# Float64 weights by bit masks and ScalarE, key moments from 512 keys, and a new table of places

## The chip, the cores and the metric

The kernel runs on one core of a Trainium2 chip (trn2) as one program. The metric is the device time of an execution in microseconds (us). Engines are PE (matmul, transposes; writes PSUM), DVE (VectorE), ACT (ScalarE), POOL (GpSimd) and SP, which here only issues DMAs. Each engine works through its own queue in order and waits on semaphores for the others.

## The reference

Attention over 8 batches x 8 heads of 576 tokens with 64 dimensions, which keeps the 32 largest scores of each row, and behind it a layer with SoLU activation. `q`, `k`, `v` and `g_ln` are float32; `w_in` (512 x 1024) and `w_out` (1024 x 512) come as float64.

```python
scores = np.matmul(q, k.transpose(0, 1, 3, 2)) / np.sqrt(64)
kth = np.partition(scores, -32, axis=-1)[..., -32:-31]
scores = np.where(scores >= kth, scores, -1e9)
attn = np.exp(scores - scores.max(-1, keepdims=True))
attn = attn / (attn.sum(-1, keepdims=True) + 1e-9)
x = np.matmul(attn, v)            # (B, H, S, D) -> (B*S, H*D) = 4608 x 512
h = x @ w_in
solu = h * softmax(h)             # over 1024
ln = (solu - solu.mean(-1)) / np.sqrt(solu.var(-1) + 1e-6) * g_ln
out = ln @ w_out
```

## The kernel before

The work is cut into 32 **pairs** (a batch and two of its heads). A pair has nine score tiles of 128 queries x 576 keys: four row blocks for each of two heads (`j` = 0 to 7), and a ninth that holds the last 64 queries of both. Behind each batch come four **token tiles** of 128 tokens, and behind every second batch a **tails tile** with the last 64 tokens of two batches: 36 tiles through both weight matrices.

For a pair, in the order of the data (engine in brackets):

- `load_qk`, `load_v` [SP] bring q, k and v; `prep_t`, `prep_m` [PE] transpose q and k, and `prep_tc`, `prep_mc` [ACT] copy them to SBUF.
- `moments` [PE] multiplies the keys by themselves in bf16: per head a 64 x 64 matrix, over four blocks of main keys and a fifth with the last 64 (`kt`). `moments_c` [ACT], `spread` [PE], `spread_v` and `spread_r` [DVE] and `first_p` [POOL, with a power of 2.2 us] make of it the spread of each query's scores, and `first` [DVE] the first guess of the threshold.
- `scores` [PE] and `evac` [ACT] put the scores into SBUF. `count0` [DVE] counts those above the guess, `second` [DVE] improves it; `count1` [ACT, a sign with an accumulator], `third` [DVE]; `count2` [ACT].
- `side`, `nearest` (a product and MAX8) and `kth` [DVE] find the 32nd largest score among the eight nearest to the last guess.
- `exps` [ACT], `keep` [DVE] and `inverse` [DVE], `norm` [POOL] make the probabilities; `transpose_p`, `transpose_last` [PE] with `copy_p`, `copy_pt`, `copy_last` [ACT], and `attn_v` [PE] with `copy_v` [ACT] the result.

A token tile goes through `mm1` [PE, two halves], `hexp` [ACT], `solu` [DVE], `square` [ACT], `ln` [POOL], `transpose_ln` [PE] and `copy_ln` [ACT], `mm2` [PE, two halves] and `store` [ACT, then SP].

The **weights** are 16 chunks of 128 x 512, eight of `w_in` and eight of `w_out`. `load_w` brings 512 KB of float64; `finish_w` is a generator whose three steps are taken one at a time (`weights_step`). In `float64_stages` DVE masks exponent (L31) and mantissa (L34), POOL scales both (L37, L40, L43); DVE adds the low word (L47), POOL multiplies (L50); DVE sets the sign (L52). A chunk of `w_out` is then multiplied by `g_ln` on POOL (L563).

The **order** is written out by hand: tables give each function a place (`pair_times` and so on), a pair's places are moved by 39 per pair, and all calls are sorted by place. That order is the program order of PE, ACT, DVE and POOL; a place is no time.

```python
    with tc.manual_schedule(engines={E.PE, E.Activation, E.DVE, E.Pool}):
        for _, _, f, args in sorted(todo, key=lambda x: x[:2]):
            f(*args)
```

Buffers that matter below: the pool `p1` holds one tile of tag `e` (`hexp`'s result, or a chunk's helper), `p2` two of `solu` (also a chunk's `w_tmp`) and two of `lnT` (also `w_raw`); `ps_big` two PSUM tiles for scores, `spread` and `mm1`.

This is the fast path. At its end sums over range tests of the intermediate values decide (`bad`) whether a **general path** computes everything again.

Of the kernel before, what the change touches and what calls it, by code (L numbers as in the profile page):

```python
# [8 lines left out]
F32 = mybir.dt.float32  # L9
I32 = mybir.dt.int32  # L10
U32 = mybir.dt.uint32
AF = mybir.ActivationFunctionType
ALU = mybir.AluOpType
AX = mybir.AxisListType

P = 128
# [427 lines left out]
def fast_path(  # L444
# [22 lines left out]
    nc = tc.nc  # L467
    B, H, S, D = q.shape
    NTOK, DM = out.shape
    DFF = moe_w_in.shape[1]  # L470
    NM = 4
    SM = NM * P
# [4 lines left out]
    NT = 2 * NM + 1  # L477
    NG = NT // 3
    SP = S // 2
    scale = 1.0 / float(D) ** 0.5  # L480
    Z0 = 1.593
# [4 lines left out]
    const = ctx.enter_context(tc.tile_pool(name="const", bufs=1))  # L486
    p1 = ctx.enter_context(tc.tile_pool(name="p1", bufs=1))
    p2 = ctx.enter_context(tc.tile_pool(name="p2", bufs=2))
# [3 lines left out]
    small = ctx.enter_context(tc.tile_pool(name="small", bufs=3))  # L492
# [21 lines left out]
    den_all = const.tile([P, NPAIR, NT], F32, tag="den", name="den_all")  # L514
    NTT = NTOK // P
    sum_all = const.tile([P, NTT], F32, tag="sum", name="sum_all")
    w_in = const.tile([P, NP, DFF], F32, tag="w_in", name="w_in")
    w_out = const.tile([P, NF, DM], F32, tag="w_out", name="w_out")
    g_rows = const.tile([NF, P], F32, tag="g_rows", name="g_rows")
# [2 lines left out]
    def trunc(ap):  # L522

        return ap.bitcast(BF16)[:, 1::2]

# [6 lines left out]
    for c in range(NF):  # L534
        w_chunks.append((w_out[:, c, :], moe_w_out[c * P : (c + 1) * P, :], c))
    w_raw = {}

    def load_g():
        nc.sync.dma_start(out=g_rows, in_=moe_g_ln.rearrange("(c p) -> c p", p=P))
# [8 lines left out]
            dst = w_raw[n]  # L548
        nc.sync.dma_start(out=dst, in_=src)

    def finish_w(n):

        dst, _, c = w_chunks[n]
        if w_wide:
            tmp = p2.tile([P, 2, 512], F32, tag="solu", name="w_tmp")
            mi = p1.tile([P, DFF], F32, tag="e", name="w_mi")
            yield from float64_stages(
                nc, dst, w_raw.pop(n), tmp[:, 0, :].bitcast(I32),
                mi[:, 0:512].bitcast(U32), tmp[:, 1, :],
            )  # L560
        if c is not None:

            nc.gpsimd.tensor_scalar(  # L563
                out=dst, in0=dst, scalar1=g_col[:, c : c + 1], scalar2=1.0,
                op0=ALU.mult, op1=ALU.mult,
            )

    w_gen = [finish_w(n) for n in range(len(w_chunks))]

    def weights_step(n):  # L570

        next(w_gen[n], None)

    st = [dict() for _ in pairs]
    xs = {}

    def once(d, key, make):

        if key not in d:
            d[key] = make()
        return d[key]

    def columns(i, tag, n=NT):

# [80 lines left out]
    def moments(i):  # L667
        d = st[i]
        tm = d["tm"] = pre_of(i)[:, 2 * ST : 2 * ST + D]
        for c in range(NM + 1):  # L670
            for h in range(2):
                kc = trunc(d["k"][:, 2 * c + h, :] if c < NM else d["kt"][:, h, :])
                nc.tensor.matmul(
                    out=tm[h * D : (h + 1) * D, :], lhsT=kc, rhs=kc,
                    start=(c == 0), stop=(c == NM),
                )

    def moments_c(i):
# [44 lines left out]
    def first_p(i):  # L723
        d = st[i]
        zs = d["zs"] = small.tile([P, NT], F32, tag="zs", name="zs")
        nc.gpsimd.tensor_scalar(
            out=zs, in0=d["ss"], scalar1=(Z0 * scale) ** 2 / S, scalar2=0.0,
            op0=ALU.mult, op1=ALU.add,
        )
        nc.gpsimd.tensor_tensor(out=zs, in0=zs, in1=phalf.broadcast_to([P, NT]), op=ALU.pow)  # L730
        d["tb"] = small.tile([P, NT], F32, tag="tb", name="tb")
        nc.gpsimd.tensor_scalar(
            out=d["tb"], in0=zs, scalar1=GAIN, scalar2=1.0, op0=ALU.mult, op1=ALU.mult
        )
# [339 lines left out]
    def at(time, f, *args):  # L1074
        todo.append((time, len(todo), f, args))


    pair_times = [
        (load_qk, [()], [-58.99]),
        (load_v, [()], [63.01]),  # L1080
        (prep_t, [()], [-29.06]),
        (prep_m, "qk", [-17.93, -25.9]),
        (moments, [()], [-24.5]),
        (prep_mc, "qk", [-16.74, -20.27]),
        (prep_tc, [()], [-18.7]),
        (moments_c, [()], [-20.21]),
        (spread, [()], [-15.63]),
        (spread_v, [()], [-15.34]),
        (spread_r, [()], [-13.06]),
        (first_p, [()], [-11.47]),  # L1090
        (first, [()], [-4.23]),
        (scores, range(5), [-12.77, -11.6, -9.27, -3.78, 1.11]),
        (evac, range(9), [-10.49, -9.85, -8.6, -8.21, -5.25, -5.03, -0.94, 3.26, 4.09]),
        (count0, range(9), [-0.65, -1.04, 5.18, 0.67, 2.49, 3.79, 5.59, 6.31, 6.49]),
        (count1, range(9), [8.67, 11.56, 8.39, 15.22, 11.55, 15.92, 8.84, 12.95, 9]),
        (count2, range(9), [24.54, 23.39, 22.97, 27.54, 22.75, 26.2, 40.38, 22.38, 24.63]),
        (second, [()], [7.56]),
        (third, [()], [19.38]),
        (exps, range(5), [46.12, 46.89, 59.29, 47.09, 49.88]),
        (side, range(3), [32.91, 35.6, 47.44]),  # L1100
        (inverse, range(3), [60.53, 62.76, 70.19]),
        (count_off, [()], [43.35]),
        (kth, [()], [56.17]),
        (nearest, range(9), [47.92, 34.61, 33.06, 53.79, 43.22, 41.09, 53.94, 47.78, 51.15]),
        (keep, range(9), [60.22, 58.49, 57.58, 61.89, 61.02, 61.33, 68.76, 65.22, 67.79]),
        (norm, range(9), [61.79, 60.82, 62.99, 71.21, 66.07, 69.03, 72.1, 75.78, 75.04]),
        (transpose_p, range(9), [63.71, 62.99, 65.75, 71.3, 67.17, 74.03, 74.35, 76.97, 78.34]),
        (copy_p, range(8), [64.96, 64.28, 69.12, 73.12, 72.01, 74.46, 78.05, 80.43]),
        (copy_pt, range(2), [81.21, 81.06]),
        (transpose_last, range(2), [83.39, 84]),  # L1110
        (copy_last, range(2), [84.33, 84.45]),
        (attn_v, range(2), [85.64, 86.38]),
        (copy_v, range(2), [86.71, 97.14]),
    ]

    token_times = [
        (mm1, range(2), [57.48, 47.95]),
        (hexp, [()], [59.95]),
        (solu, [()], [60.57]),
        (square, [()], [63.1]),  # L1120
        (ln, [()], [64.54]),
        (transpose_ln, range(2), [65.72, 67.37]),
        (copy_ln, range(2), [68.41, 72.58]),
        (mm2, range(2), [100.41, 103.28]),
        (store, [()], [113.91]),
    ]

    tails_times = [
        (mm1, range(2), [60.95, 53.05]),
        (hexp, [()], [64.35]),  # L1130
        (solu, [()], [64.75]),
        (square, [()], [81.91]),
        (ln, [()], [86.34]),
        (transpose_ln, range(2), [86.8, 110.93]),
        (copy_ln, range(2), [86.92, 112.35]),
        (mm2, range(2), [112.01, 113.68]),
        (store, [()], [122.85]),
    ]

    last_times = [  # L1140
        (mm1, range(2), [63.4, 58.32]),
        (hexp, [()], [80.96]),
        (solu, [()], [81.36]),
        (square, [()], [82.63]),
        (ln, [()], [85.89]),
        (transpose_ln, range(2), [100.26, 106.23]),
        (copy_ln, range(2), [112.23, 110.59]),
        (mm2, range(2), [128.53, 139.72]),
        (store, [()], [140.88]),
    ]  # L1150

    load_w_times = [
        -47.88, -331.05, -24.69, -10.07, 55.47, 65.78, 165.31, 124.24, -12.29, 19.64, 117.51,
        83.89, 148.52, 166.47, 210.46, 225.81,
    ]
    weights_times = [
        -9.25, 0.94, 7.94, -220.27, -175.79, -9.1, 2.37, 12.12, 12.53, 27.92, 37.21, 55.4,
        80.95, 96.19, 109.13, 92.63, 95.65, 108.24, 192.81, 199.17, 206.1, 160.16, 160.24,
        185.05, 15.23, 22.24, 52.22, 72.58, 77.56, 84.13, 120.85, 130.1, 154.08, 124.04, 148.6,
        151.85, 170.38, 171.77, 179.42, 198.66, 201.86, 209.49, 211.67, 227.23, 232.91, 241.34,  # L1160
        252.44, 256.85,
    ]

    at(-135.57, load_g)
    for n in range(len(w_chunks)):
        at(load_w_times[n], load_w, n)
        for time in weights_times[3 * n : 3 * n + 3]:
            at(time, weights_step, n)

    def all_times(base, table, *first):  # L1170
        for f, args, times in table:
# [36 lines left out]

    ok = small.tile([P, 5], F32, tag="ok", name="ok")
    hit = p2.tile([P, NPAIR, NT], F32, tag="w", name="hit")
    for n, (a, lim, op) in enumerate((
        (zk_all, 1e-12, ALU.is_gt), (den_all, 1.0, ALU.is_ge), (den_all, 1e30, ALU.is_le),
        (sum_all, 1.0, ALU.is_ge), (sum_all, 1e30, ALU.is_le),
    )):
        nc.vector.tensor_scalar(
            out=hit if n < 3 else hit[:, 0:4, :].rearrange("p a b -> p (a b)")[:, 0:NTT],
            in0=a, scalar1=lim, scalar2=None, op0=op, op1=ALU.add, accum_out=ok[:, n : n + 1],
        )  # L1220
    tp = ps_tp.tile([P, NM, P], F32, tag="tp", name="tp_ok")
    nc.tensor.matmul(out=tp[0:1, 0, 0:5], lhsT=ones, rhs=ok, start=True, stop=True)
    n_ok = small.tile([1, 1], F32, tag="n_ok", name="n_ok")
    nc.vector.tensor_reduce(out=n_ok, in_=tp[0:1, 0, 0:5], axis=AX.X, op=ALU.add)
    nc.vector.tensor_scalar(
        out=bad, in0=n_ok, scalar1=P * (3.0 * NPAIR * NT + 2.0 * NTT) - 0.5, scalar2=None,
        op0=ALU.is_lt,
    )

# [42 lines left out]
```

## Time and profile before

| What | Value |
|---|---|
| Median of 3 runs | 1353.24 us (1353.04 to 1353.94) |
| The profiled execution's own time | 1353.02 us |
| Its span, first to last instruction | 1351.2 us |
| PE busy | 1213.3 us (90%) |
| DVE busy | 1171.6 us (87%) |
| ACT busy | 1135.5 us (84%) |
| POOL busy | 565.6 us (42%) |
| Mean granted PE clock | 0.952 |

The span lies inside the time; the 1.8 us around it are start and end of the execution. A busy share is a mean over stages: this kernel has an entry, a stage in which the weights are converted, a long run of alike pairs, and an end with token tiles alone, and each has to be read by itself. In a line of groups, `x` is how many instructions there were, then come their busy time, the mean of one in ns, and the idle time of the engine ahead of them with what ended it. Records can overlap by some .08 us, so from start to start an instruction often takes less than its own length.

### The profile page before, as it was taken

To read this page: it belongs to the slowest core of one execution; us is meant where nothing else is said; L and a number is where in the kernel's file an instruction comes from. 1 tells how busy PE (TensorE), PEld (TensorE's weight loads), DVE (VectorE), ACT (ScalarE), POOL (GpSimd) and SP (SyncE) were. 2 spreads that over 40 slices of the span, in tenths; PEclk is the share of its full clock that TensorE was granted. 3 is DMA by queue.
4 is the path that set the end of the run, shared out by engine and by line. 5 is a ranking of instruction groups with operands and counts; after the bars stand their busy time and mean duration, and the time that the engine had idled before them with its cause. 6 is when DMAs were issued, how large, how long until landed. Compare 5 with 4: busy or idle time off the path is not lost.

```text
span 1351.2 us, 20257 instructions
## 1 busy us (share of the span) xinstructions
PE 1213.3 (90%) x6307; PEld 657.0 (49%) x6307; DVE 1171.6 (87%) x2780; ACT 1135.5 (84%) x2622; POOL 565.6 (42%) x614
## 2 busy tenths in 40 slices
PE   6476558989999999999999999999999999999997
PEld 3243334545555545555555545555555555545443
DVE  4899999999999989899999989899999989899110
ACT  4877777889999989899999989899999989896231
POOL 6477766644444413334444423234444433134120
PEclk9687668899999999999999999999999999999999
DMA  5111111101111110111111111111111111000001
GB/s 140 52 41 50 49 49 49 44 19 34 36 36 36 29 36 27 35 35 36 28 36 37 36 28 34 37 36 28 34 35 28 36 28 36 25 17 8 16 8 34
DMA packets 102405, 48.60 MB, mean 36 GB/s; under 512 B 87432, under 2 KB 95632, under 8 KB 102288
## 3 DMA queue, kind: packets, MB, share of 16 engines
q1 hardware_dynamic: 102288, 47.21, 12.9%
q8 instruction: 53, 0.87, 0.3%
q14 instruction: 64, 0.52, 0.1%
HBM read 37.75 MB, written 9.44 MB: 35 GB/s over the span
## 4 chain that ended last, share of the span: by engine, by line
DVE 50%; PE 21%; ACT 16%; issue 6%; POOL 5%; DMA 0%; SPq 0%; DVEq 0%; POOLq 0%; ACTq 0%
DVE w L855 10%; DVE w L860 10%; DVE E L897 9%; DVE junkv L788 8%; PE h_ps L1000 6%; PE o_ps L1058 6%; ACT junka L804 5%; PE s_ps L771 4%; POOL E L912 2%; ACT E L868 2%; PE om L978 2%; ACT sg L834 2%; DVE solu L1019 2%; PE tp_p L926 2%; DVE Et L897 2%
## 5 line engine op out<-in xcount | busy, mean ns | idle before, releaser
L1058 PE MATMUL o_ps<-w_out,lnT 128*128 128x512 f32 x576 | 260.0, 596 | 0.9 <-ACT xTt L992 0.8
L912 POOL TENSOR_SCALAR E<-E,rden 128x576 f32<-128x576 f32 x256 | 234.3, 926 | 63.1 <-DVE rden L908 34.0
L771 PE MATMUL s_ps<-qkT 64*128 64x288 f32 (+1 forms) x1280 | 238.7, 459 | 11.3 <-ACT X L780 10.4
L1000 PE MATMUL h_ps<-w_in,xTm 128*128 128x512 f32 x512 | 237.4, 608 | 2.7 <-ACT xTm L989 2.7
L860 DVE MAX8 w<-w 128x8 f32<-128x576 f32 x288 | 219.2, 761 | 9.9
L897 DVE SCALAR_TENSOR_TENSOR E<-X,kth,E 128x576 f32<-128x576 f32 x256 | 221.0, 891 | 4.0
L827 POOL TENSOR_SCALAR tt<-t 128x9 f32<-128x9 f32 x32 | 21.3, 667 | 481.4 <-DVE t L821 481.3
L804 ACT ACTIVATE junka<-X,t 128x576 bf16<-128x576 f32 x256 | 196.5, 779 | 26.5 <-DVE t L798 26.5
L855 DVE SCALAR_TENSOR_TENSOR w<-X,al,sg 128x576 f32<-128x576 f32 x256 | 213.1, 832 | 2.5 <-DVE al L843 0.2
L834 ACT ACTIVATE sg<-X,t 128x576 bf16<-128x576 f32 x256 | 199.2, 800 | 8.5 <-DVE t L821 8.4
L788 DVE TENSOR_SCALAR_CACHE_REDUCE junkv<-X,t 128x576 bf16<-128x576 f32 x256 | 194.6, 803 | 11.8 <-ACT X L780 11.8
L926 PE MATMUL tp_p<-ident,E 128*128 128x128 f32 x1024 | 155.8, 289 | 49.6 <-POOL E L912 47.1
L780 ACT ACTIVATE X<-s_ps 128x576 f32<-128x576 f32 x256 | 158.3, 660 | 41.0 <-PE s_ps L771 39.1
L938 ACT COPY PT<-tp_p 128x512 f32<-128x512 f32 x256 | 146.5, 598 | 34.1 <-PE tp_p L926 33.9
L771 PEld LDWEIGHTS s_ps<-qkT 64*128 64x128 f32 (+1 forms) x1280 | 129.7, 190 | 90.0 <-ACT X L780 34.3
L926 PEld LDWEIGHTS tp_p<-ident,E 128*128 128x128 f32 x1024 | 115.4, 145 | 100.2 <-POOL E L912 76.0
L1058 PEld LDWEIGHTS o_ps<-w_out,lnT 128*128 128x128 f32 x576 | 105.5, 191 | 112.5 <-issue 109.9
L1000 PEld LDWEIGHTS h_ps<-w_in,xTm 128*128 128x128 f32 x512 | 93.4, 191 | 111.8 <-issue 105.7
L868 ACT ACTIVATE E<-X 128x1152 f32<-128x1152 f32 x128 | 144.8, 1213 | 0.0
L978 PE MATMUL om<-PT,vm 128*64 128x288 f32 x1024 | 138.3, 412 | 0.0
L978 PEld LDWEIGHTS om<-PT,vm 128*64 128x64 f32 x1024 | 67.8, 136 | 57.3 <-issue 18.8
L730 POOL TENSOR_TENSOR zs<-zs,phalf 128x9 f32<-128x9 f32 x32 | 70.1, 2191 | 2.7
(128 smaller groups left out, 1673.3 us busy)
## 6 DMA issues: line engine op xcount, KB each, us to landing
qm<-in_q_dram SPq DMA_DIRECT2D x32, 256.0 KB, 3.3
km<-in_k_dram SPq DMA_DIRECT2D x32, 256.0 KB, 3.2
vm<-in_v_dram SPq DMA_DIRECT2D x32, 256.0 KB, 2.8
out_dram<-osb SPq DMA_DIRECT2D x32, 256.0 KB, 2.3
w_raw<-in_moe_w_in_dram SPq DMA_DIRECT2D x8, 512.0 KB, 3.9
w_raw<-in_moe_w_out_dram SPq DMA_DIRECT2D x8, 512.0 KB, 3.6
qt<-in_q_dram SPq DMA_DIRECT2D x32, 32.0 KB, 2.2
kt<-in_k_dram SPq DMA_DIRECT2D x32, 32.0 KB, 2.7
```

The costliest lines, as they stand in the source:

```text
L771: nc.tensor.matmul(out=s[:, half, 0:SH], lhsT=qkT[hd, qs], rhs=qkT[hd, k0 : k0 + SH], start=True, stop=True,)
L788: nc.vector.tensor_scalar(out=junk, in0=x_of(i, j), scalar1=d["t0"][:, j : j + 1], scalar2=None, op0=ALU.is_ge, op1=ALU.add, accum_out=col ...
L804: nc.scalar.activation(out=junk, in_=x_of(i, j), func=AF.Sign, scale=-1.0, bias=d["t1"][:, j : j + 1], accum_out=columns(i, "n1")[:, j : j ...
L834: nc.scalar.activation(out=d["sg", j], in_=x_of(i, j), func=AF.Sign, scale=-(1.0 + 2.0**-23), bias=d["t2"][:, j : j + 1], accum_out=column ...
L855: nc.vector.scalar_tensor_tensor(out=w, in0=x_of(i, j), scalar=d["al"][:, j : j + 1], in1=d.pop(("sg", j)), op0=ALU.subtract, op1=ALU.mult,)
L860: nc.vector.max(w8[:, j, :], w)
L897: nc.vector.scalar_tensor_tensor(out=e, in0=x_of(i, j), scalar=d["kth"][:, j : j + 1], in1=e, op0=ALU.is_ge, op1=ALU.mult, accum_out=den_a ...
L912: nc.gpsimd.tensor_scalar(out=e, in0=e, scalar1=st[i]["rden"][:, j : j + 1], scalar2=1.0, op0=ALU.mult, op1=ALU.mult,)
L926: nc.tensor.transpose(tp[:, c, :], e[:, c * P : (c + 1) * P], ident)
L978: nc.tensor.matmul(out=o[h * D : (h + 1) * D, 0:SP], lhsT=vm[:, h, c, :] if c < NM else vt[hd, :], rhs=pt[:, h * NM + c, :] if c < NM else ...
L1000: nc.tensor.matmul(out=h[:, half, :], lhsT=x[:, c, :], rhs=w_in[:, c, half * 512 : (half + 1) * 512], start=(c == 0), stop=(c == NP - 1),)
L1058: nc.tensor.matmul(out=o, lhsT=d["lnT"][:, c, :], rhs=w_out[:, c, :], start=(c == 0), stop=(c == NF - 1),)
```

## The change

A chunk's conversion becomes six calls with places of their own: `w_bits` on DVE (three instructions: the high word shifted and masked to a float32 `val`, its sign and top bit set, and its power of two `power` cut out), `w_low` on ACT (the low word scaled by 2^-52), `w_mul` and `w_add` on POOL (low word times power, plus `val`), `w_gain` on POOL (only `w_out`), and `w_check` on ACT (three instructions, which count for each partition the high words within a range). The counts go into `w_ok`, which a sixth range test reads at the end. The moments leave the `kt` block out, and `first_p` divides by 512 instead of 576. All tables of places are new.

```diff
+    def w_bits(n):
+        tmp = w_tmp[n] = p2.tile([P, 2, 512], F32, tag="solu", name="w_tmp")
+        val, power = tmp[:, 0, :].bitcast(U32), tmp[:, 1, :].bitcast(U32)
+        nc.vector.tensor_scalar(
+            out=val, in0=words(n, 1), scalar1=3, scalar2=0x3FFFFFFF,
+            op0=ALU.logical_shift_left, op1=ALU.bitwise_and,
+        )
+        nc.vector.scalar_tensor_tensor(
+            out=val, in0=words(n, 1), scalar=0xC0000000, in1=val,
+            op0=ALU.bitwise_and, op1=ALU.bitwise_or,
+        )
+        nc.vector.tensor_scalar(
+            out=power, in0=val, scalar1=0xFF800000, scalar2=None, op0=ALU.bitwise_and
+        )
+    def low_of(n):
+        return once(w_tmp, ("low", n), lambda: p1.tile([P, 2, 512], F32, tag="e", name="w_low"))
+    def w_low(n):
+        nc.scalar.activation(
+            out=low_of(n)[:, 0, :], in_=words(n, 0), func=AF.Copy, scale=2.0**-52
+        )
+    def w_check(n):
+        f = low_of(n)[:, 1, :]
+        nc.scalar.activation(
+            out=f, in_=words(n, 1).bitcast(I32), func=AF.Square, scale=2.0**-27
+        )
+        nc.scalar.activation(out=f, in_=f, func=AF.Square, bias=m65)
+        nc.scalar.activation(
+            out=f, in_=f, func=AF.Sign, scale=-1.0, bias=p251, accum_out=w_ok[:, n : n + 1]
+        )
+    def w_mul(n):
+        low = low_of(n)[:, 0, :]
+        nc.gpsimd.tensor_tensor(out=low, in0=low, in1=w_tmp[n][:, 1, :], op=ALU.mult)
+    def w_add(n):
+        nc.gpsimd.tensor_tensor(
+            out=w_chunks[n][0], in0=w_tmp[n][:, 0, :], in1=low_of(n)[:, 0, :], op=ALU.add
+        )
...
-            yield from float64_stages(
-                nc, dst, w_raw.pop(n), tmp[:, 0, :].bitcast(I32),
-                mi[:, 0:512].bitcast(U32), tmp[:, 1, :],
-            )
...
-        for c in range(NM + 1):
+        for c in range(NM):
...
-            out=zs, in0=d["ss"], scalar1=(Z0 * scale) ** 2 / S, scalar2=0.0,
+            out=zs, in0=d["ss"], scalar1=(Z0 * scale) ** 2 / SM, scalar2=0.0,
...
-        (second, [()], [7.56]),
-        (third, [()], [19.38]),
+        (second, [()], [10.45]),
+        (third, [()], [21.53]),
...
     tails_times = [
-        (mm2, range(2), [112.01, 113.68]),
+        (mm2, range(2), [109.69, 122]),
...
-        (sum_all, 1.0, ALU.is_ge), (sum_all, 1e30, ALU.is_le),
+        (sum_all, 1.0, ALU.is_ge), (sum_all, 1e30, ALU.is_le), (w_ok, 511.5, ALU.is_ge),
```

In each engine's queue the parts of a pair stay in the same sequence of functions, while single tiles trade places. These moves matter most: in front of `third` the new DVE queue has four `nearest`, `kth` and four `keep` where there were five `nearest`, `kth` and one `keep`, and behind it come three more `keep` ahead of `solu`; ACT has all four `exps` of a pair ahead of `count1`; on PE `transpose_p` 8 follows the last `scores`, and of the tails tile's `mm2` the second half comes behind those `scores` instead of ahead of them. On SP's queue a second weight chunk stands ahead of the first q and k.

## The prediction

> **What bounds the kernel now.** I read the windows first, cut at the start of each pair's last `kth` instruction (L889): from one start to the next is one period, one pair of heads. The columns are busy us of each engine, then the granted clock.
>
> ```profile
> 65.20:104.90 39.70, 25.04 (x152) 15.45 (x152) 38.66 (x89) 32.60 (x78) 28.73 (x24) 0.76 0.17 51
> 188.90:233.20 44.30, 34.91 (x168) 18.75 (x168) 43.24 (x93) 32.04 (x75) 29.45 (x27) 0.76 0.20 57
> 346.60:382.60 36.00, 34.69 (x193) 18.76 (x192) 34.80 (x84) 34.73 (x82) 14.29 (x16) 1.00 0.13 34
> 490.60:532.90 42.30, 42.06 (x223) 22.85 (x223) 35.72 (x90) 37.26 (x85) 14.95 (x19) 1.00 0.14 36
> 532.90:572.60 39.70, 38.53 (x204) 20.55 (x202) 35.04 (x85) 33.38 (x78) 13.90 (x16) 1.00 0.11 29
> 1240.30:1351.20 110.90, 102.19 (x331) 49.16 (x329) 19.92 (x61) 30.37 (x60) 20.03 (x27) 0.98 0.05 18
> ```
>
> Five stages stand there. Entry, to 65.2. Weights, 65.2 to 310.5: six periods, 245.3 us in all, DVE full (39 of 40) while ACT has 7 to 12 us free in each. Steady: three times five periods of 36.0, DVE without a wait; its 34.8 busy and 1.2 of small gaps are the period. Bumps: three groups of three periods (42.3 + 39.7 + 38.4 = 120.4, so 12.4 over 108), where a tails tile is extra and PE is full. Exit, where PE works without a pause to the end. The chain agrees:
>
> ```profile
> DVE 50%; PE 21%; ACT 16%; issue 6%; POOL 5%; DMA 0%; SPq 0%; DVEq 0%; POOLq 0%; ACTq 0%
> ```
>
> Then the groups of instructions, for the price of a chunk (out<-in, count | busy, mean ns of one):
>
> ```profile
> L31 DVE TENSOR_SCALAR w_tmp<-w_raw 128x512 int32<-128x512 int32 x16 | 7.5, 466 | 6.5 <-DMA w_raw<-in_moe_w_in_dram 4.7 <-DMA w_raw<-in_moe_w_out_dram 1.9
> L34 DVE TENSOR_SCALAR w_mi<-w_raw 128x512 uint32<-128x512 uint32 x16 | 8.6, 537 | 0.0
> L47 DVE SCALAR_TENSOR_TENSOR w_tmp<-w_raw,w_tmp 128x512 f32<-128x512 uint32 x16 | 11.4, 719 | 0.8 <-POOL w_tmp L37 0.8
> L52 DVE SCALAR_TENSOR_TENSOR w_out<-w_raw,w_tmp 128x512 uint32<-128x512 uint32 x8 | 5.6, 705 | 0.0
> L40 POOL TENSOR_SCALAR w_tmp<-w_tmp 128x512 int32<-128x512 int32 x16 | 32.4, 2026 | 1.3
> L50 POOL TENSOR_TENSOR w_tmp<-w_tmp 128x512 f32<-128x512 f32 x16 | 23.4, 1462 | 8.8 <-DVE w_tmp L47 7.6 <-DVE u L796 0.7
> L938 ACT COPY PT<-tp_p 128x512 f32<-128x512 f32 x256 | 146.5, 598 | 34.1 <-PE tp_p L926 33.9
> ```
>
> **Weights stage.** A chunk costs DVE .466 + .537 + .719 + .705 = 2.43 now. After: two masks like L31 (.466 each; no row has the two-operation or the contiguous form, which are bounded by .42, the fastest L31, and .54, L34) and one like L52 (.705): 1.64. In the new order 11 chunks stand behind the first `kth` (9, 4, 5, 10, 11, 7, 12, 6, 13, 14, 15); 44 instructions stand there before. 11 x .79 = 8.7 us saved on the engine that is full.
>
> A second gain is POOL's. Six steady periods of DVE, less the token work that the first four lack (4 x 1.5 = 6), are 202.8; the 44 weight instructions take 23.6 by start to start; DVE was busy 239.0. The other 12.6 us are ordinary DVE instructions that ran slower beside a POOL that was busy 155 us, not 86. POOL's part of a chunk falls from .78 + 2.03 + 2.03 + 1.46 = 6.3 to two TENSOR_TENSORs, 2.9 by L50: about half of its excess, so some 6 us of the 12.6. DVE alone would end the stage 14.7 earlier.
>
> ACT is the price. `w_low`, two squares and a sign: the nearest copy starts every .48 (L938 back to back), a 576-wide sign with its accumulator every .76 (ten records of L804 in 3.79 us), so .5 + .5 + .5 + .7 = 2.2; double for the two that read 8-byte steps gives 3.2. 11 x 2.2 = 24 on top of 196.8 makes 221 of the 230.6 us that DVE would leave: 96%, where a steady period has 34.7 of 36. It fits, but hardly: `low_of` has one buffer, so `w_low` or `w_check` of a chunk waits for POOL's `w_add` of the chunk before, and evacuations stand behind it in ACT's queue, for which `count0` on DVE waits. One such wait of .8 us in each period gives back 4.7. I take -10, between -14.7 and 0.
>
> Here a rule speaks against the change. Row: L34 takes .42 undisturbed (its median .423) and .537 in the mean, so collisions cost .12 each; 33 masks cost 4 us, which the means above already hold. The Trainium skill, "SBUF — State Buffer", section "Who interferes with whom", says that a VectorE tensor_scalar in a 2-port mode, or an instruction with two SBUF inputs, and a GpSimd instruction block each other wholly, in order of issue. By it, each mask could wait out a whole `w_mul`: at most 33 x 1.46 = 48 us; I keep the row.
>
> **Entry.** SP's queue now issues a second 512 KB chunk ahead of `qm` and `km` (before it stood behind them). The first 12 us moved 190 GB/s in the mean with peaks near 330: 1.6 to 2.8 us later for `km`, on which the first `prep` waits. Q is transposed first now, and two moment matmuls go; DVE loses three weight instructions between 39.7 and 65.2 (1.8), and idles 20.7 before. ACT's five new chunks (11 us) lie in its gaps before evacuations (1.5 us each at half clock), all but about .5; a gap missed costs a chunk's 2.2. Net +1, from -1 to +4.
>
> **Steady.** No row changes here but four `kt` matmul records (2 per pair, .22 each, PE is not the bound) and `zs`. What changes is the order, so which DVE instructions meet POOL:
>
> ```profile
> 952.41 0.81 DVE L897 SCALAR_TENSOR_TENSOR E<-X,kth,E 128x576 f32<-128x576 f32 x1
> 953.14 1.29 DVE L897 SCALAR_TENSOR_TENSOR E<-X,kth,E 128x576 f32<-128x576 f32 x1
> 957.69 1.29 DVE L897 SCALAR_TENSOR_TENSOR Et<-Xt,kth,Et 128x576 f32<-128x576 f32 x1
> 963.29 0.56 DVE L740 TENSOR_TENSOR t<-mean,zs 128x9 f32<-128x9 f32 x1
> 963.96 0.61 DVE L742 SCALAR_TENSOR_TENSOR ta<-tb,t 128x9 f32<-128x9 f32 x1
> ```
>
> A `keep` is .81 alone and 1.29 when a `norm` on POOL has started; `t` and `ta`, .17 at the start of the run, are .56 and .61. That is .48 + .48 + .39 + .44 = 1.8 us in every period. In the new order `third` and three keeps follow the first `inverse` directly, where `solu` (one operand in PSUM, not slowed) stood beside two norms; I count one more collision, less what the shorter list before `first16` saves: +.3 per period, between -1.8 and +1.5. 15 x .3 = +4.5. Laid end to end, the new ACT queue still has its first `count1` ready within 3 us of slack on both sides, and `first` still comes after `first_p`, by half a us where it was 1.7.
>
> **Bumps.** In the second period DVE waits for evacuation 7, because both halves of the tails tile's `mm2` stand ahead of the last scores:
>
> ```profile
> DVE junkv L788 <- ACT X L780: 3.4, 1, 3.4
> DVE yq L710 <- PE y_ps L692: 2.4, 1, 2.4
> ```
>
> The new order puts one half (8 x .43 = 3.4 us) behind `scores` 4. The wait goes; PE is late then by 3.4 at the next `spread`, for which it has some 3 us in the new order. PE's own work sets the floor: 42.1 + 38.5 + 37.8 less 6 x .22. I take -3 for each group, from 0 to -3.5: -9 in three. The first period stays: four halves of `mm1` and one of `mm2` still stand ahead of its `spread`.
>
> **Exit.** The same PE work, still with three or more half tiles between each `mm1` and its transposes (10 us against 6.5 of exp, solu, square and `ln` by their rows), and the sixth range test takes .4 of the 25.4 us that DVE waits for PE at the end: 0.
>
> **Sum.** +1 - 10 + 4.5 - 9 = -13.5 from the profiled 1353.0 (span 1351.2 and 1.8 around it), which is 0.2 under the median of 1353.24: 1339.7.
>
> **Rivals.** (1) Slower: the lock between `norm` and two-operand DVE instructions. If the new order costs each steady period the upper bound, 1.5 instead of .3, the sum is +4.5: 1357.7. It decides from 1.2 per period on, a period of 37.2. For it: `third` and keeps now meet the first norms; against: counts and MAX8, which POOL doesn't slow, are still most of DVE's row. (2) ACT becomes the bound of the weights stage, its gain is 0: 1349.7. For it: 96%; against: the half-clock scores leave ACT idle there anyway. (3) PE only moves its backlog, the bumps give 2 (the `kt` records): 1346.7. (4) Gains and costs cancel within 0.2%. (5) It doesn't do what it says: a failed test on `w_ok`, or a threshold from 512 keys that lands too far off, starts the general path: 288 tiles x four MAX8 of .76 alone are 875 us more, over 2200. Worked from the inputs, all weights are far inside (largest .216), and the count is within 13 of 513 in every row where 15 is the limit; only a conversion that ScalarE does otherwise would do it.
>
> **Chances.** Forecast .46, (1) .20, (2) .15, (3) .10, (4) .07, (5) .02. A change of 0.2%, 2.7 us, is what a measurement of this kernel can tell. Faster: .46 + .15 + .10 = .71; same .07; slower .22. Low end: ACT keeps up (-4.7), the steady order costs nothing (-4.5) and its collisions fall by .3 per period (-4.5): 1326. High end: rival (1), 1358.
>
> **What would show it.** Right: six weights periods near 39.2 in the mean, ACT over 36 busy in them; steady periods of 36 to 36.5; the 3.4 wait gone. Wrong: steady periods over 37 with more keeps at 1.29, or ACT waiting on POOL's `w_add`.

## The result, and the profile after

The changed kernel takes 1353.8 us in the median (1352.5 to 1354.2), the kernel before 1353.4: ratio 1.0001, 95% interval 0.9984 to 1.0018. Its profiled execution takes 1354.09 us, with a span of 1352.3. So nothing was won or lost that a measurement can tell, where 13.5 us less were forecast. The windows of the changed kernel, cut as before at the start of each pair's last `kth` instruction (now L934), show that a great deal moved all the same. Columns: busy us of PE, its weight loads, DVE, ACT and POOL, then the granted clock, DMA share and GB/s.

```profile
67.20:105.80 38.60, 26.00 (x150) 14.86 (x150) 37.46 (x87) 36.41 (x85) 16.86 (x17) 0.80 0.15 46
188.70:230.60 41.90, 31.74 (x161) 17.94 (x162) 40.73 (x89) 38.76 (x90) 22.64 (x22) 0.76 0.15 42
344.00:380.80 36.80, 35.53 (x192) 19.40 (x191) 35.69 (x85) 34.71 (x82) 13.40 (x16) 1.00 0.12 33
491.20:531.40 40.20, 39.61 (x207) 21.59 (x206) 36.62 (x88) 35.47 (x83) 15.35 (x19) 1.00 0.11 29
531.40:568.50 37.10, 37.10 (x197) 20.24 (x198) 35.98 (x85) 31.98 (x74) 13.39 (x16) 1.00 0.13 32
568.50:607.50 39.00, 38.41 (x203) 20.94 (x202) 35.07 (x85) 38.44 (x93) 13.39 (x16) 1.00 0.15 39
```

The first two are periods of the weights stage: POOL is down from 28 or 29 us to 17 to 23, ACT is up from 32 to between 36 and 39. The third is a steady period, and the reader should stay with it: 36.8 where it was 36.0, with DVE busy 35.7 where it was 34.8. DVE has the same work there. The last three are a bump group, 42.3 + 39.7 + 38.4 before, 40.2 + 37.1 + 39.0 now. DVE still holds half of the chain of work that ended last; PE has 27% of it where it had 21%, and POOL, 5% before, is gone from it:

```profile
DVE 52%; PE 27%; ACT 12%; issue 6%; DVEq 0%; ACTq 0%
```

In the groups (count | busy, mean ns of one) the new conversion stands as follows; the first three are `w_bits`, then `w_low` and the sign of `w_check`:

```profile
L579 DVE TENSOR_SCALAR w_tmp<-w_raw 128x512 uint32<-128x512 uint32 x16 | 9.6, 602 | 7.2 <-DMA w_raw<-in_moe_w_in_dram 7.2
L583 DVE SCALAR_TENSOR_TENSOR w_tmp<-w_raw,w_tmp 128x512 uint32<-128x512 uint32 x16 | 14.3, 892 | 0.5
L587 DVE TENSOR_SCALAR w_tmp<-w_tmp 128x512 uint32<-128x512 uint32 x16 | 8.4, 526 | 0.5
L595 ACT ACTIVATE w_low<-w_raw 128x512 f32<-128x512 uint32 x16 | 10.7, 670 | 3.3 <-DMA w_raw<-in_moe_w_in_dram 3.1 <-POOL w_in L614 0.2
L605 ACT ACTIVATE w_low<-w_low,p 128x512 f32<-128x512 f32 x16 | 11.6, 722 | 0.6
```

A chunk's `w_bits` is .602 + .892 + .526 = 2.02, not 1.64. Why steady periods grew is seen in the timeline of one of them (start, length; all on DVE), 681.6 to 718.4:

```profile
685.66 0.64 DVE L866 TENSOR_SCALAR t<-t 128x9 uint32<-128x9 uint32 x1
687.68 1.29 DVE L942 SCALAR_TENSOR_TENSOR E<-X,kth,E 128x576 f32<-128x576 f32 x1
693.83 0.36 DVE L888 SCALAR_TENSOR_TENSOR al<-n,tt 128x3 f32<-128x3 f32 x1
694.23 1.28 DVE L900 SCALAR_TENSOR_TENSOR w<-X,al,sg 128x576 f32<-128x576 f32 x1
698.00 0.62 DVE L888 SCALAR_TENSOR_TENSOR al<-n,tt 128x3 f32<-128x3 f32 x1
```

and beside it on POOL (L957 is `norm`):

```profile
685.52 0.74 POOL L957 TENSOR_SCALAR E<-E,rden 128x576 f32<-128x576 f32 x1 [20.26 <-DVE step L858]
694.16 0.75 POOL L957 TENSOR_SCALAR E<-E,rden 128x576 f32<-128x576 f32 x1
```

In a steady period of the kernel before, `third`'s mask, a `nearest` product and a `side` that ran while POOL had no norm took:

```profile
948.80 0.17 DVE L821 TENSOR_SCALAR t<-t 128x9 uint32<-128x9 uint32 x1
966.76 0.81 DVE L855 SCALAR_TENSOR_TENSOR w<-X,al,sg 128x576 f32<-128x576 f32 x1
974.60 0.16 DVE L843 SCALAR_TENSOR_TENSOR al<-n,tt 128x3 f32<-128x3 f32 x1
```

Now `third`'s mask (L866) starts .14 behind a norm and ends .04 behind that norm's end. A `nearest` product (L900) starts .07 behind a norm and takes 1.28. By start to start, a steady period changed by: `third`'s mask +.47, `nearest` +.47, `side` (L888) +.55, against -.48 for a second `keep` that no longer meets a norm and -.2 of small ones: +.8.

### The profile page after: what moved, and what is told of

It is laid out like the page before. It is cut to its first block, busy times and chain, and to the rows that moved or that the text cites. A ratio compares the mean times of both kernels' runs of the same rounds, so it can differ in the third digit from the quotient of the medians.

```text
span 1352.3 us, 20269 instructions
## 1 busy us (share of the span) xinstructions
PE 1231.0 (91%) x6243; PEld 672.3 (50%) x6243; DVE 1183.2 (87%) x2766; ACT 1174.3 (87%) x2702; POOL 486.7 (36%) x584
## 4 chain that ended last, share of the span: by engine, by line
DVE 52%; PE 27%; ACT 12%; issue 6%; DVEq 0%; ACTq 0%
DVE w L900 11%; DVE w L905 10%; DVE E L942 10%; PE o_ps L1103 8%; PE h_ps L1045 8%; DVE junkv L833 8%; ACT junka L849 4%; PE om L1023 3%; PE s_ps L816 3%; DVE solu L1064 2%; PE tp_p L971 2%; ACT sg L879 2%; DVE al L888 1%; ACT PT L983 1%; ACT X L825 1%
## 5 line engine op out<-in xcount | busy, mean ns | idle before, releaser
L957 POOL TENSOR_SCALAR E<-E,rden 128x576 f32<-128x576 f32 x256 | 239.3, 945 | 602.9 <-DVE step L858 496.6
L816 PE MATMUL s_ps<-qkT 64*128 64x288 f32 (+1 forms) x1280 | 259.1, 467 | 22.5 <-ACT X L825 11.6
L900 DVE SCALAR_TENSOR_TENSOR w<-X,al,sg 128x576 f32<-128x576 f32 x256 | 220.9, 863 | 1.1
L942 DVE SCALAR_TENSOR_TENSOR E<-X,kth,E 128x576 f32<-128x576 f32 x256 | 212.2, 875 | 4.1 <-ACT junka L849 0.9
L816 PEld LDWEIGHTS s_ps<-qkT 64*128 64x128 f32 (+1 forms) x1280 | 143.1, 192 | 106.6 <-ACT X L825 38.4
L971 PE MATMUL tp_p<-ident,E 128*128 128x128 f32 x1024 | 159.9, 293 | 13.2 <-POOL E L957 5.6
L913 ACT ACTIVATE E<-X 128x1152 f32<-128x1152 f32 x128 | 153.6, 1250 | 0.1
L983 ACT COPY PT<-tp_p 128x512 f32<-128x512 f32 x256 | 143.3, 606 | 7.8 <-PE tp_p L971 7.7
L971 PEld LDWEIGHTS tp_p<-ident,E 128*128 128x128 f32 x1024 | 117.0, 147 | 64.2 <-issue 20.2
L1056 ACT ACTIVATE e_sb<-h_ps 128x1024 f32<-128x1024 f32 x36 | 38.2, 1062 | 41.3 <-PE h_ps L1045 41.3
L1061 DVE RECIPROCAL rs<-sum_all 128x1 f32<-128x1 f32 x36 | 5.6, 156 | 64.7 <-ACT e_sb L1056 64.4
```

Of the source, the lines that this page charges most:

```text
L816: nc.tensor.matmul(out=s[:, half, 0:SH], lhsT=qkT[hd, qs], rhs=qkT[hd, k0 : k0 + SH], start=True, stop=True,)
L900: nc.vector.scalar_tensor_tensor(out=w, in0=x_of(i, j), scalar=d["al"][:, j : j + 1], in1=d.pop(("sg", j)), op0=ALU.subtract, op1=ALU.mult,)
L942: nc.vector.scalar_tensor_tensor(out=e, in0=x_of(i, j), scalar=d["kth"][:, j : j + 1], in1=e, op0=ALU.is_ge, op1=ALU.mult, accum_out=den_a ...
L957: nc.gpsimd.tensor_scalar(out=e, in0=e, scalar1=st[i]["rden"][:, j : j + 1], scalar2=1.0, op0=ALU.mult, op1=ALU.mult,)
L971: nc.tensor.transpose(tp[:, c, :], e[:, c * P : (c + 1) * P], ident)
```

## Experiments

Behind "Measured" stand the median time of all executions and its ratio to the kernel before. Periods, stages, spans and waits are read from the profiled execution, cut in stages as the prediction cut them; the exit in the table takes in the short last period (28.7 before) ahead of the prediction's exit. The two halves of the change, its functions and its tables, were first put alone.

**The tables of before with the new functions.** `pair_times`, `token_times`, `tails_times` and `last_times` are those of the kernel before; `weights_times` with the new calls stays. Two of the lines, against the changed kernel:

```diff
...
-        (second, [()], [10.45]),
-        (third, [()], [21.53]),
...
+        (second, [()], [7.56]),
+        (third, [()], [19.38]),
...
```

> The changed kernel's conversion, check and 512-key moments, with the four tables of pairs and tiles of the kernel before. Theory (the order causes the dearer steady period, by meetings of POOL's norm with DVE): steady period 36.0 (36.8 in the changed kernel), three bump periods 120.4 as before, weights stage (second 1 to second 7) 246.6 - 12 = 235, entry some 4 later, span about 1343. Rival (the conversion or the moments make the steady period dearer): steady period stays 36.8. Rival (ACT bounds the weights stage): stage 243 or more.

**The new tables with the functions of before.** The same four tables the other way round; two of the lines, against the kernel before:

```diff
...
-        (second, [()], [7.56]),
-        (third, [()], [19.38]),
...
+        (second, [()], [10.45]),
+        (third, [()], [21.53]),
...
```

> The kernel before with only the four tables of pairs and tiles of the changed kernel; conversion, its places and the 576-key moments as before. Theory (order): steady period 36.8, bump groups 116 to 117, weights stage 246.6 + 5 = 251, entry within 1 of before; span about 1351 + 13 - 11 + 5 = 1358. Rival (conversion or moments): steady 36.0 and span no longer than 1346.

Measured: 1361.1 us for the new functions alone, ratio 1.0053 (1.0036 to 1.0070), and 1361.7 for the new order alone, ratio 1.0057 (1.0040 to 1.0074).

| Stage | before | new order alone | new functions alone | both |
|---|---|---|---|---|
| entry | 65.2 | 63.4 | 69.4 | 67.2 |
| weights, 6 periods | 245.4 | 250.5 | 250.7 | 239.6 |
| steady, 15 periods | 540.7 | 553.8 | 540.4 | 554.1 |
| bumps, 9 periods | 360.4 | 350.3 | 360.9 | 349.1 |
| exit | 139.6 | 142.2 | 139.9 | 142.3 |
| span | 1351.2 | 1360.2 | 1361.2 | 1352.3 |

Each half alone costs 9 or 10 us in these spans (7 to 8 in the median times); together they cost 1. The new order costs the steady periods 13.1 and the weights stage 5.1, and gives 10.1 in the bumps. (Some 1.7 of its entry and exit only shift the cut: `kth` now follows `second` sooner.) The functions, in the new order, take 10.9 off the weights stage (250.5 to 239.6). In the old order they add 5.3 to it, against the expectation. So the halves don't add, and what either is worth in this stage depends on which of them is put in first. Waits of DVE in the weights stage, first with the new functions alone, then with the new order alone:

```profile
DVE step L858 <- ACT junka L849: 4.4, 2, 2.4
DVE rs L1061 <- ACT e_sb L1056: 3.8, 2, 2.3
```

```profile
DVE w_out L52 <- POOL w_tmp L50: 2.0, 1, 2.0
DVE w_tmp L47 <- POOL w_tmp L37: 1.6, 2, 0.8
```

In the old order DVE now waits 8.2 for `count1` and `hexp` on ACT, whose queue has the new work in it: there ACT holds up DVE, as rival (2) had it for this stage. In the new order, with the functions, the list of DVE's waits for that stage is empty. The second pair of lines, 3.6 of waiting for POOL between the steps of one chunk, goes with the old functions. It is most of the 5.1 that the new order alone costs this stage; DVE's instructions account for some 1.6 (`third`'s masks take 2.5 more, other small ones give part of it back).

**The norms behind `solu`.** If steady periods are longer because `norm` meets `third` and `keep`, then `hexp` and `solu` put where the norms begin should bring them back:

```diff
-        (inverse, range(3), [60.22, 65.15, 70.68]),
+        (inverse, range(3), [60.6, 65.15, 70.68]),
...
-        (norm, range(9), [61.06, 60.35, 61.47, 67.95, 65.36, 69.22, 73.72, 72.19, 78.35]),
+        (norm, range(9), [61.06, 60.62, 61.47, 67.95, 65.36, 69.22, 73.72, 72.19, 78.35]),
...
-        (hexp, [()], [61.29]),
-        (solu, [()], [63.24]),
+        (hexp, [()], [60.62]),
+        (solu, [()], [60.65]),
```

> The changed kernel with four places moved: inverse 0 behind third, solu right behind it and ahead of three keeps, and so the first norms start beside solu, which has only one operand in SBUF. Theory (each meeting of a norm and a DVE instruction that uses the shared way to SBUF costs DVE .48): third's mask .55 to .08 and the keep of 1.22 to .74, steady period 36.8 - .95 = 35.9, span 1352 - 14 = 1338. Rival (the period is set by PE or by ACT waiting for DVE, the meetings are hidden): steady stays 36.5 or more.

Measured: 1348.2 us, ratio 0.9960 (0.9946 to 0.9975). A steady period takes 36.24, .56 less; not 35.9, since one collision was traded in:

```profile
609.55 0.17 DVE L866 TENSOR_SCALAR t<-t 128x9 uint32<-128x9 uint32 x1
612.33 1.21 DVE L942 SCALAR_TENSOR_TENSOR E<-X,kth,E 128x576 f32<-128x576 f32 x1
616.56 0.93 DVE L950 TENSOR_SCALAR rden<-den_all 128x3 f32<-128x3 f32 x1
```

The mask is short again, a `keep` still meets the second norm, and the second `inverse`, a matter of .16, now waits for the token tile's `ln` on POOL. By start to start: mask -.47, `nearest` -.43, `side` -.29, `inverse` +.77. The steady periods give 10.4 in all, but the bumps take 6.0 back (349.1 to 355.1): their third period has DVE waiting 5.2 for ACT, 2.7 at `third` as in the changed kernel and 2.5 at `solu`.

**One norm left out.** `norm` returns at once for tile 4 of each pair, so these probabilities aren't divided by their sum:

```diff
     def norm(i, j):
+        if j == 4:
+            return
```

> The changed kernel without norm on tile 4 of each pair (these probabilities aren't divided by their sum; nothing else is left out). Theory (a two-input DVE instruction runs .48 longer beside a norm): the nearest that stood beside this norm takes .80 instead of 1.28, and a steady period falls by about .5, from 36.8 to 36.3; POOL's busy time falls by 1.5 a period. Rival (the longer nearest is hidden, PE or ACT sets the period): steady stays within .15 of 36.8.

Measured: 1343.9 us, ratio 0.9927 (0.9910 to 0.9943); a steady period takes 36.06, .74 less. The `nearest` that met this norm gives .44; `side` gives .30, since `first_p` and the norms behind it come .75 sooner on POOL. So one norm, .74 long, costs DVE .74 where it stands. The timeline of a steady period has that `nearest` as

```profile
651.83 0.84 DVE L900 SCALAR_TENSOR_TENSOR w<-X,al,sg 128x576 f32<-128x576 f32 x1
```

**Without the range test on ACT.** `w_check` isn't called and a memset on POOL sets `w_ok`, so the weights' range isn't tested:

```diff
-    if not w_wide:
-        nc.gpsimd.memset(w_ok, 512.0)
+    nc.gpsimd.memset(w_ok, 512.0)
...
-        (w_check, w_wide, range(NW), [
+        (w_check, False, range(NW), [
```

> The changed kernel without w_check: the count of in-range weights is set, not computed, so 48 ACT instructions (some 27 us of ACT) go. Theory (DVE bounds the weights stage; ACT's new load is hidden there but not in the entry): weights stage 239.6 within 1.5, entry (to second 1) 60.1 - 2 = 58, steady 36.8, span about 1349.5. Rival (ACT holds the weights stage): stage 233 to 236.

Measured: 1350.1 us, ratio 0.9974 (0.9963 to 0.9985). Weights 239.1, where they were 239.6: ACT, though busy 224.7 of 239.6 us with the test, doesn't hold this stage. The entry falls by 2.2.

**The first loads.** The load of chunk 0 goes behind the first q and k, its `w_bits` behind the first `spread`:

```diff
         (load_w, True, range(NW), [
-            -87.15, -415.46, -43.63, -12.61, 21.87, 64.19, 175.15, 128.59, -37.12, 34, 73.87,
+            -56.0, -415.46, -43.63, -12.61, 21.87, 64.19, 175.15, 128.59, -37.12, 34, 73.87,
...
         (w_bits, w_wide, range(NW), [
-            -60.89, -367.77, -0.85, 14.29, 80.61, 99.69, 186.71, 139.22, 16.19, 70.02, 111.85,
+            -12.4, -367.77, -0.85, 14.29, 80.61, 99.69, 186.71, 139.22, 16.19, 70.02, 111.85,
```

> The changed kernel with two places altered: the load of weight chunk 0 stands behind the first q and k on SP's queue (as before the change), and w_bits of chunk 0 behind the first spread's instructions on DVE. Theory (SP's queue holds part of the entry: with the second 512 KB ahead, k lands about 2 us later and all of the first pair with it): entry to the second of pair 1 falls from 60.1 to about 57.5, all other stages as in the changed kernel, span about 1349.5. Rival (the five new chunks on ACT ahead of the evacuations set the entry, whenever k lands): entry stays within 1 us of 60.1, span 1352.

Measured: 1350.7 us, ratio 0.9978 (0.9969 to 0.9988). In the changed kernel the first transposes wait for `qm` until 9.02, with this edit until 5.76; the two lines are PE's timelines of the one and of the other:

```profile
9.02 1.12 PE L697 MATMUL tp_qk<-ident,qm 128*128 128x128 f32 x4 [4.42 <-DMA qm<-in_q_dram]
```

```profile
5.76 1.12 PE L697 MATMUL tp_qk<-ident,qm 128*128 128x128 f32 x4 [0.94 <-DMA qm<-in_q_dram]
```

The entry, 67.2, becomes 64.2; to the `second` of pair 1, the cut that the expectation uses, 60.1 becomes 57.1. The weights stage stays (239.5). The theory holds: 3.0 of the entry are SP's order (with the `w_bits` that moved along with it). The test on ACT was the cause of another part (2.2 where it was left out); the two edits weren't run together.

**One half of `mm2` back ahead of the last scores:**

```diff
-        (mm2, range(2), [109.69, 122]),
+        (mm2, range(2), [109.69, 116.3]),
```

> The changed kernel with one place altered: the second half of the tails tile's mm2 stands directly ahead of scores 4 instead of behind them (PE has the same work). Theory (the bumps' gain is this half out of the way of the last scores): evacuation 7 and what waits for it come 3.4 us later, DVE waits some 3 us again, and three bump periods take 119.5 instead of 116.3, the span 1361. Rival (the gain is the missing kt matmuls and the shorter first guess, not this place): bumps stay at 116.3 to 117, span 1352.

Measured: 1356.3 us, ratio 1.0020 (1.0010 to 1.0029). The wait is back in the second bump period:

```profile
DVE junkv L833 <- ACT Xt L825: 3.1, 1, 3.1
```

but a bump group takes 117.4, not 119.5: the second period gains 3.2 (37.1 to 40.3) and the third loses 2.1 (39.0 to 36.9), where a wait of 2.7 falls to .6. So the place is worth 1.1 for each group, not 3. Most of the wait isn't removed by it, but handed to the next period:

```profile
DVE step L858 <- ACT junka L849: 2.7, 1, 2.7
```

(the changed kernel's third bump period). Where the rest of the gain came from is seen by counting PE's instructions by period: cut at `second`, the three bump periods hold 102 `attn_v` matmuls where they held 120, and the period behind them 56 where it held 40. PE is behind by 16 to 18 matmuls when the group ends, and makes it up in a period that is DVE's (37.3, where the next ones take 36.8). Taken over four periods, a group and the one behind it, the old kernel needs 156.4 and the new one 153.6. The missing `kt` matmuls are only a small part of that: the new order with the old functions, which still has them, counts the same 102 and 56 and needs 154.2, so they give some .6, and in the three periods of a group .4 (350.3 to 349.1 in three groups).

**The edits of the order together.** The norms behind `solu` and the first loads as above, with the second `inverse` moved ahead of `keep` 7, and the changed kernel's places of `hexp` and `solu` for the second token tile behind a tails tile. What is new against those two runs:

```diff
-        (inverse, range(3), [60.6, 65.15, 70.68]),
+        (inverse, range(3), [60.6, 63.7, 70.68]),
...
-                all_times((n + t) * STEP, token_times, d)
+                all_times((n + t) * STEP, late_times if t == 1 and b in (2, 4, 6) else token_times, d)
```

> The changed kernel with the norms moved behind hexp and solu (as in the earlier run), the second inverse moved ahead of keep 7, the old places of hexp and solu kept for the second token tile behind each tails tile, and the load of chunk 0 behind q and k. Theory (the collisions of DVE with norm and ln, the late hexp in the third bump period, and SP's order are separate and add up): steady periods 35.9, so 15 x .9 = 13.5 less than the changed kernel; bumps 116.5 each; entry 57.5; weights 239.6; span 1336 to 1341. Rival (each removed collision only moves to the next instruction of DVE, since POOL runs a norm in 40% of every period): steady stays at 36.2, span 1344 or more.

Measured: 1344.6 us, ratio 0.9934 (0.9917 to 0.9951). Steady 36.18, nearly as the rival has it: the `inverse` is short again, which is worth .77, but by start to start the `nearest` that meets a norm is 1.31 and `side` .52 again. (Norms take 8.3 of a steady period in the changed kernel, 23%, not 40%.) Bumps 115.8, and 37.8 in the period behind each group. The weights stage takes 242.6.

**The same without moving the second `inverse`** (against the run before):

```diff
-        (inverse, range(3), [60.6, 63.7, 70.68]),
+        (inverse, range(3), [60.6, 65.15, 70.68]),
```

> As the run that combined the edits, but with the second inverse left in the changed kernel's place. Theory (moving that inverse made nearest meet the norm behind it, and cost the weights stage 3): weights 239.6 again, steady 36.24 as with the norms behind solu alone, entry 57.1, bumps 115.8 and 1.6 in the period behind each; span about 1340, 2 less than the combined run. Rival (the 3 in the weights stage come from chunk 0's later conversion): weights stay at 242.6 and the span at 1342.5 or more.

Measured: 1340.8 us (1340.2 to 1340.9), ratio 0.9905 (0.9890 to 0.9920): the fastest of all, .95% ahead of both kernels. Weights 239.9, steady 36.2:

```profile
405.70:441.90 36.20, 35.08 (x192) 19.10 (x190) 35.14 (x84) 34.80 (x81) 13.01 (x16) 1.00 0.13 34
```

The extra 3 in the weights stage were the moved `inverse`, not chunk 0's later conversion.

**One more collision taken away**, from the run that put the edits together: norm 4 behind `first_p`, `transpose_p` 4 behind the scores that follow it:

```diff
-        (norm, range(9), [61.06, 60.62, 61.47, 67.95, 65.36, 69.22, 73.72, 72.19, 78.35]),
+        (norm, range(9), [61.06, 60.62, 61.47, 67.95, 66.2, 69.22, 73.72, 72.19, 78.35]),
...
-            63.34, 62.61, 66.09, 69.24, 66.67, 70.76, 74.72, 77.24, 79.13,
+            63.34, 62.61, 66.09, 69.24, 69.0, 70.76, 74.72, 77.24, 79.13,
```

> The run that combined the edits, with norm 4 moved behind first_p on POOL and transpose_p 4 behind the scores that follow it on PE. Theory (POOL then runs first_p, whose long power slows no DVE instruction, while DVE is in the first nearest and the second side): nearest .83 instead of 1.31 and side .2 to .3 less, steady 35.5 instead of 36.18, so 9 to 10 less in 15 periods; span about 1333. Rival (norm 4 only meets the next two-input instruction, or PE waits for the later transposes): steady 36.0 or more, span 1340 or more.

Measured: 1377.7 us, ratio 1.0178 (1.0164 to 1.0192). The windows show that DVE did become faster: 34.0 busy in a steady period, where the run that put the edits together had 35.1. But the period is 36.7, the bumps are 365.1 in all and the weights stage 246.9:

```profile
376.99:413.65 36.66, 35.31 (x192) 19.42 (x194) 34.00 (x85) 34.58 (x82) 12.29 (x16) 1.00 0.12 33
```

```profile
DVE rs L1061 <- ACT e_sb L1056: 3.1, 2, 1.5
```

DVE now waits 1.5 in every period for `hexp`, which comes late. ACT's only wait in such a period is at the copy of tile 4, for the transposes that this edit put back:

```profile
ACT PT L983 <- PE tp_p L971: 1.9, 1, 1.9
```

Its 34.6 busy and these 1.9 make 36.5 of the 36.7, so ACT sets the period here. With PE 35.3 and ACT 34.6 busy, a period has little room below 36 us, however fast DVE is; no steady period of these runs is below 36.0.

## Why the prediction was wrong, point by point

The span was forecast to fall by 13.5 and rose by 1.1. The step that failed most is the price of the new order for a steady period: +.3 was taken ("one more collision"), +.8 was measured, and with 1.3 more in single periods the fifteen cost 13.4 instead of 4.5. The second is the price of `w_bits`, taken at 1.64 a chunk and measured at 1.95 by start to start, so that the chunks saved 2.1 on DVE where 8.7 were forecast.

- **Steady: +13.4, forecast +4.5.** The prediction saw that the new order decides which DVE instruction meets `norm`, and for the new order counted one more collision of `keep`'s size. A `keep` collision in fact went (-.48), while the mask, `nearest` and `side` together cost 1.5 more. The prediction had itself priced `t` and `ta`, tiny instructions at .56 and .61, but didn't ask which other tiny ones the new order would bring there: `third`'s mask (one input, 128 x 9), `side` and, in a later run, `inverse` (128 x 3) pay for the rest of POOL's norm or `ln` whatever their size. Some 12.0 of the 13.4 are this (15 x .8); the rest stands in the period behind each bump group (37.3, PE's backlog) and in a few periods of 37.1, which weren't traced. Rival (1), which decides "from 1.2 per period", named the right mechanism; its +1.5 was not reached.
- **Weights: -5.8, forecast -10.** By start to start, the 44 old weight instructions took 23.6 in this stage and the 33 new ones take 21.5. The two-input one of `w_bits` is the most above its price: .892 in the mean, where .705 was taken and its median is .694. Ordinary DVE instructions give 3.8 where some 6 were forecast; the forecast's 4.7 for waits on ACT was not needed. In the new order the functions alone give 10.9. That this is near the forecast's 10 is luck, as the parts are others: 2.3 from the chunks' instructions, some 5.2 from ordinary ones beside a less busy POOL (`keep` -3.7, `nearest` -2.0, some others longer) and 3.4 from waits that go.
- **A full block was weighed there and not taken:** if each mask waited out a whole `w_mul`, 48 us would be lost. The 22 masks take .51 from start to start in this stage, .42 undisturbed, so 2 us; the 11 two-input instructions lose another 2 (.892 against .694). The rule of the Trainium skill, "SBUF — State Buffer", section "Who interferes with whom", is seen where the two do meet: `third`'s mask ends with its norm. Here the sequence of instructions decides how often they meet.
- **Entry: +2.0, forecast +1.** The functions cost 3.8 there (63.4 to 67.2), out of SP's order and the test on ACT; the new order gives 1.8, most of it the cut. Without that shift the entry is some 3.7 dearer; up to the `second` of pair 1 it grew from 54.9 to 59.9.
- **Bumps: -11.3, forecast -9,** near by luck, as the account was wrong. The 3.4 wait went, but its place brings only 1.1 of the 3.8 that a group gained, and the missing `kt` matmuls .4. The remaining 2.3 come with the other moves of the order. They fit PE's backlog carried over the group's end (16 to 18 `attn_v` matmuls, which start every .136, are 2.2 to 2.4 us), which was counted, but not tried by itself. "The first period stays" was wrong: 42.3 became 40.2.
- **Exit: +2.7, forecast 0,** of which some 1.7 is the shifted cut; the other 1.0 comes with the new order (.9 where it stands alone), and why wasn't traced.
- **The likeliest case.** What came true was rival (4), "gains and costs cancel", with a chance of .07; the time lies within the range.

## What to carry to other kernels

When a new order changes which instructions of two engines run side by side, price it in every stage that runs this order, and count all instructions that can meet the other engine, small ones first: their own length says nothing of what a meeting costs. A step that is off the bound in one stage can be paid back in the next: a cheaper DVE period lost 6 of 10 us to the bumps, which are PE's, and a wait removed from one period turned up in the following one. Before two parts of a change are added, ask whether one was made for the other: here each alone cost 7 to 10 us, and both together some 1.

## What the runs showed of the hardware

- A one-input DVE instruction on 128 x 3 or 128 x 9 elements, .16 and .17 alone, took .93 beside POOL's `ln` and .64 beside a `norm`.
- A `nearest` product of 128 x 576, .80 alone, that started .07 behind a norm ended .60 behind the norm's end; one that ran inside POOL's power on 128 x 9 elements (1.81 long in the changed kernel) took .79.
- ACT reads 128 x 512 words at 8-byte steps in .67 and .68 (L595, L601); the contiguous square and sign take .72. The prediction had allowed up to twice the time for the steps.
- With a second 512 KB load ahead of it on SP's queue, the first transposes of `qm` started 3.3 us later (9.02 against 5.76).
